# Attention with two feed-forward layers on one core: the softmax is moved from SBUF into the scores' PSUM banks

## Chip, core and metric

The kernel runs on one NeuronCore of a Trainium2 chip. The metric is the device time of one execution in microseconds (us). The engines are named as in the profile: PE is TensorE (matmuls; PEld is its loading of weights), DVE is VectorE, ACT is ScalarE, POOL is GpSimd and SP is SyncE, which here only issues DMAs. SBUF is the working memory that every engine reads; PSUM holds what PE writes, in eight banks of 512 fp32 columns for each of the 128 partitions. DVE and ACT can read and write PSUM. In this kernel POOL only ever touches SBUF.

## What is computed

```python
scores = q @ k.T / sqrt(64)                     # 4 x 8 heads, 576 x 576 each
cum = cumsum(log(clip(f, 1e-4, 1)))
scores = where(causal, -1e9, scores + cum[:, None] - cum[None, :])
attn = exp(scores - scores.max(-1)) ; attn /= attn.sum(-1) + 1e-9
x = (attn @ v) laid out as 2304 tokens x 512
x = leaky(x @ w_in) @ w_out                     # first layer, hidden 2048
h = x @ w2_in ; h = h * softmax(h)              # second layer, hidden 1024
out = (layernorm(h) * g_ln) @ w2_out
```

fp32 operands that are multiplied are split in a high and a low part, so that most products are three matmuls. The attention weights are split in fp16 the same way: `hl` holds the high and the low part of a block's rows.

## The kernel before

The 32 heads are worked in 16 pairs. Each head's scores fall into query blocks of 128 rows, 0 to 3, with 128, 256, 384 and 512 keys (causal); the last 64 rows of both heads of a pair make up a fifth block of 576 keys (`scores4`, block 4). Pairs 0 to 3 are done in two goes (blocks 0 and 1, then 2 to 4); pairs 4 to 15 in one go.

`scores` and `softmax` do one unit of blocks after the other; `UNITS` says which blocks share a unit. For each block PE writes scores into a bank `ps_s` (there are four). DVE adds the mask, takes the row maximum (L676, L695 for block 4) and writes the result to an SBUF tile `sd`, of which there are also four. From there all of it is in SBUF: ACT takes the exponential in place and its row sum (L641), a small instruction adds 1e-9 and scales (L649 on ACT, L651 on DVE or POOL), DVE takes the reciprocal (L654), and then come two large pieces per block:

```python
copy_f(hl.t[:, ho:ho + w], sd..., engs=HI_ENGS, scale=rs)    # high part, L425 ACT or L432 POOL
sub_f(hl.t[:, lo:lo + w], sd..., hl.t[:, ho:ho + w],
      engs=LO_ENGS if prio < LOP else ("DVE",), scale=rs)    # low part, L436 DVE or L439 + L440 POOL
```

A DMA transposes the unit's `hl` into `pt`, and PE multiplies it with the values (`ps_v`). ACT and DVE scale the result and add its two parts into `xr` (L706, L709). Around this run the preparation of keys and queries (`kq`, mostly POOL), of values (`VT`) and of weights (`wk`, four DVE instructions for each 128 x 512 chunk).

The first feed-forward layer is worked in nine token blocks. Its first half (`ffn_a`, nine hidden units of 12 matmuls each per token block, with g at L822 to L824) is interleaved with the attention as soon as a token block's attention output is there; the rest (`ffn_b`, `layer2`) follows.

Nothing of the order is decided on the chip. A planner (`Plan.run`) goes through all operations with costs written in the code, picks for each engine the operation of the best priority that is ready by those costs, chooses between engines where several are allowed, and hands out buffers. Each engine then executes its list in that order, and waits where an input or a buffer is late.

Of the kernel before, what the change touches and what calls it, by code (L numbers as in the profile page):

```python
# [24 lines left out]
PT = 4  # L25
# [29 lines left out]
LOP = 310.01  # L55
# [14 lines left out]
PS = 2.0 ** -15  # L70
# [25 lines left out]
HEAT = 0.25  # L96
# [260 lines left out]
def body(tc, kqa, kq, vt, f, one, wa, w2i, w2o, gln, out):  # L357
    nc = tc.nc
    es = ExitStack()
    P = Plan()  # L360
    PE, ACT, DVE, POOL, SP, CTL = "PE", "ACT", "DVE", "POOL", "SP", "CTL"
# [23 lines left out]
    ap = attn.enter_context(tc.tile_pool(name="attn", bufs=1))  # L385
# [168 lines left out]
    st, QK, VT, U, QA = {}, {}, {}, {}, {}  # L554
# [69 lines left out]
    def qk_mm(Q, full, i, o, hd, k0, k1, first, last):  # L624
        _, qk, col = Q
        c0 = col[i]
        if full:
            a = qk(hd)
            mm(o, a[0:66, c0:c0 + 128], a[0:66, k0:k1], first, last)
            return  # L630
        a, b = qk(hd)
        mm(o, a[:, c0:c0 + 128], a[:, k0:k1], first, False)
        mm(o, b[0:68, c0:c0 + 128], b[0:68, k0:k1], False, last)

    def softmax(parts, prio):
# [17 lines left out]
        flex(REC_ENGS, [{ACT: 100.0, DVE: 70.0, POOL: 165.0}[e] for e in REC_ENGS], guard, prio, w=[(sts, 3)], r=[(sts, 2)])  # L653
        P.op(DVE, 75, lambda: nc.vector.reciprocal(sts.t[:, 6:6 + nb], scale()), prio, w=[(sts, 4)], r=[(sts, 3)])  # L654
        for sd, _, j, W, pieces in parts:
            rs = lambda j=j: sts.t[:, 6 + j:7 + j]
# [89 lines left out]
    def pair(p, prio, blocks=(0, 1, 2, 3, 4)):  # L746
# [365 lines left out]
```

## Time and profile before

| | us |
|---|---|
| median of 3 runs | 887.11 (885.61 to 887.39) |
| the profiled execution | 887.7 |
| its span, first to last instruction | 885.9 |
| PE busy | 792.5 |
| DVE busy | 611.3 |
| ACT busy | 462.3 |
| POOL busy | 419.2 |

The span is what the trace covers; the profiled execution's own time is 1.8 us longer. A busy share over the whole span mixes an attention stage (to about 385 us, when the last `xr` is written) with feed-forward stages in which PE is busy nearly all the time.

### The profile page before, as it was taken

What the parts mean: (1) busy time and instruction counts of PE and PEld (TensorE: products, weight loads), DVE (VectorE), ACT (ScalarE), POOL (GpSimd) and SP (SyncE); (2) the same over time, 40 slices, a digit from 0 to 9 for tenths busy, and PEclk for the clock granted to TensorE, in tenths of its full rate; (3) what the DMA queues carried; (4) which work ended last, traced back from release to release, by engine and by line L of the source; (5) the groups of instructions that cost most, each with busy time, mean ns of one, the idle gap of its engine ahead of it and who ended that gap; (6) DMA issues with size and microseconds to landing.
All of it is one profiled execution on the core that took longest, in us unless ns stands there. A gap on an engine that the chain in (4) does not pass through costs nothing.

```text
span 885.9 us, 15864 instructions
## 1 busy us (share of the span) xinstructions
PE 792.5 (89%) x5648; PEld 711.0 (80%) x5648; DVE 611.3 (69%) x1369; ACT 462.3 (52%) x1150; POOL 419.2 (47%) x475
## 2 busy tenths in 40 slices
PE   2576688888689889999999989999999999999997
PEld 2333487788579878999999989889889988998985
DVE  6999988999899999958947896424533354234651
ACT  4776586776778878844435444333433342323421
POOL 5888886787676776233302345121412142223321
PEclk9999999999589999999999999999999999999999
DMA  7889569987878897855532532311422141203113
GB/s 214 208 193 222 153 169 184 199 212 166 202 179 194 179 222 200 155 165 167 178 110 87 164 119 60 79 41 60 86 56 62 36 107 36 60 30 80 24 36 95
DMA packets 181961, 114.98 MB, mean 130 GB/s; under 512 B 147030, under 2 KB 163054, under 8 KB 181850
## 3 DMA queue, kind: packets, MB, share of 16 engines
q1 hardware_dynamic: 181882, 113.97, 52.8%
q8 instruction: 44, 0.72, 0.3%
q14 instruction: 35, 0.29, 0.1%
HBM read 64.32 MB, written 15.16 MB: 90 GB/s over the span
## 4 chain that ended last, share of the span: by engine, by line
PE 45%; DVE 16%; issue 4%; ACT 4%; DMA 4%; POOL 1%; SPq 0%; DVEq 0%; ACTq 0%; POOLq 0%
PE ps_f L471 27%; PE ph L471 10%; PE py L471 6%; DVE hl L436 4%; DMA tr<-hl 2%; DVE wk L779 1%; DVE g L824 1%; DVE sd L676 1%; DVE xr L709 1%; PE ps_v L471 1%; DVE wk L781 1%; PE ps_s L471 1%; DMA raw<-w2o 1%; DVE wk L776 1%; ACT sd L641 1%
## 5 line engine op out<-in xcount | busy, mean ns | idle before, releaser
L436 DVE SCALAR_TENSOR_TENSOR hl<-sd,st,hl 128x512 f16<-128x512 f32 (+4 forms) x140 | 125.0, 907 | 8.4 <-POOL hl L432 6.0
L471 PE MATMUL ps_f<-x,wi 128*128 128x256 f32 x972 | 127.8, 287 | 1.6 <-DVE g L824 1.4
L471 PE MATMUL ps_f<-g,wo 128*128 128x256 f32 x972 | 126.1, 286 | 1.8 <-DVE g L824 1.8
L471 PEld LDWEIGHTS ps_f<-x,wi 128*128 128x128 f32 x972 | 122.9, 192 | 3.7 <-DVE g L824 2.5
L471 PEld LDWEIGHTS ps_f<-g,wo 128*128 128x128 f32 x972 | 121.6, 191 | 2.9 <-DVE g L824 2.5
L641 ACT ACTIVATE sd<-sd,st 128x128 f32<-128x128 f32 (+4 forms) x144 | 83.3, 579 | 41.8 <-DVE st L676 32.4
L471 PE MATMUL ps_f<-x,wib 128*128 128x256 f32 x756 | 99.0, 282 | 2.7 <-DVE g L824 1.4
L471 PE MATMUL ph<-wi,g 128*128 128x512 f32 x408 | 98.3, 397 | 0.0
L471 PEld LDWEIGHTS ps_f<-x,wib 128*128 128x128 f32 x756 | 93.1, 189 | 4.1 <-DVE g L824 2.7
L471 PE MATMUL ps_s<-kq 68*128 68x288 f32 (+9 forms) x304 | 70.4, 357 | 27.0 <-DVE st L676 21.0
L471 PEld LDWEIGHTS <-VT 128*128 128x128 f16 x928 | 56.6, 109 | 45.1 <-issue 32.1
L471 PE MATMUL ps_v<-pt,VT 128*128 128x128 f16 (+1 forms) x928 | 65.3, 233 | 30.7 <-DVE xr L709 24.6
L822 ACT ACTIVATE g<-ps_f 128x256 fp32r<-128x256 f32 x144 | 54.3, 377 | 70.7 <-PE ps_f L471 70.1
L471 PEld LDWEIGHTS ph<-wi,g 128*128 128x128 f32 x408 | 76.1, 189 | 17.5
L471 PE MATMUL ps_f<-wo,x 128*128 128x512 f32 x348 | 84.0, 397 | 0.2 <-ACT x L425 0.2
L824 DVE TENSOR_TENSOR g<-ps_f,g 128x256 fp32r<-128x256 f32 x144 | 60.0, 417 | 34.1 <-ACT ps_f L823 32.7
L471 PEld LDWEIGHTS ps_s<-kq 128*128 128x128 f32 (+1 forms) x304 | 50.1, 209 | 35.6 <-DVE st L676 25.8
L440 POOL TENSOR_TENSOR kq<-raw,kq 64x576 fp32r<-64x576 f32 (+2 forms) x47 | 76.1, 1619 | 4.9 <-ACT kq L425 2.2
L471 PE MATMUL py<-g,wob 128*128 128x256 f32 x567 | 76.7, 280 | 1.5 <-DVE yo L900 1.5
L471 PEld LDWEIGHTS ps_f<-wo,x 128*128 128x128 f32 x348 | 64.8, 189 | 15.3 <-ACT x L425 0.4
L471 PEld LDWEIGHTS py<-g,wob 128*128 128x128 f32 x567 | 72.5, 188 | 3.6 <-ACT wk L775 1.7
L432 POOL TENSOR_SCALAR hl<-sd,st 128x128 f16<-128x128 f32 (+3 forms) x69 | 40.2, 588 | 51.6 <-DVE st L654 27.1
(147 smaller groups left out, 1363.3 us busy)
## 6 DMA issues: line engine op xcount, KB each, us to landing
raw<-kq SPq DMA_DIRECT2D x24, 608.0 KB
wst<-wa SPq DMA_DIRECT2D x17, 512.0 KB
raw<-wa SPq DMA_DIRECT2D x15, 512.0 KB
xw<-xs_d SPq DMA_DIRECT2D x24, 256.0 KB
yp_d<-yo SPq DMA_DIRECT2D x36, 128.0 KB
yw<-yp_d SPq DMA_DIRECT2D x18, 256.0 KB
out<-ot SPq DMA_DIRECT2D x18, 256.0 KB
vr<-vt SPq DMA_DIRECT2D x13, 320.0 KB
```

Of the source, the lines that this page charges most:

```text
L432: nc.gpsimd.tensor_scalar(o, i, 1.0 if scale is None else scale, 1.0, op0=ALU.mult, op1=ALU.mult)
L436: nc.vector.scalar_tensor_tensor(o, a, scale, b, op0=ALU.mult, op1=ALU.subtract)
L440: (nc.vector if eng == DVE else nc.gpsimd).tensor_tensor(o, a, b, op=ALU.subtract)
L471: nc.tensor.matmul(o, lhsT=l, rhs=r, start=start, stop=stop)
L641: P.op(ACT, act(W, 2), lambda sd=sd, j=j, W=W: nc.scalar.activation(sd.t[:, 0:W], sd.t[:, 0:W], AF.Exp, bias=sts.t[:, j:j + 1], scale=-1.0 ...
L676: P.op(DVE, dve(W) + 12, lambda i=i, j=j, W=W, ps=ps, sd=sd: nc.vector.tensor_tensor_reduce(sd.t[:, 0:W], ps.t[:, 0:W], mask[:, 384 - 128 ...
L709: P.op(DVE, dve(n) + 60, lambda: nc.vector.scalar_tensor_tensor(xr.t[a:a + 64, dst0:dst0 + n], ps.t[a:a + 64, c0:c1], u.t[a:a + 64], xr.t[ ...
L776: P.op(DVE, dve2(512), lambda: nc.vector.tensor_scalar(kf(), kf(), F64_LO, F64_HI, op0=ALU.max, op1=ALU.min), prio, rw=[k])
L779: P.op(DVE, dve(512), lambda: nc.vector.scalar_tensor_tensor(k.t, word(1), -0x40000000, k.t, op0=ALU.bitwise_and, op1=ALU.bitwise_or), pri ...
L781: P.op(DVE, dve(512), lambda: nc.vector.scalar_tensor_tensor(k.t, word(0), 29, k.t, op0=ALU.logical_shift_right, op1=ALU.bitwise_or), prio ...
L822: P.op(ACT, act(n, 0, True), lambda: nc.scalar.activation(g.t[:, 0, 0:n], h(), AF.Prelu, alpha=0.01), eprio, w=[(g, 0)], r=[ps])
L824: P.op(DVE, dve(n) + 60, lambda: nc.vector.tensor_tensor(g.t[:, 1, 0:n], h(), g.t[:, 0, 0:n].bitcast(F32), op=ALU.subtract), eprio, w=[(g, ...
```

## The change

The masked scores stay in their `ps_s` bank, and mask, exponential, high part and low part all read them there. Since POOL is left out, the high part can go to ACT or DVE and the low part to DVE alone. Blocks 0, 1 and 2 become one unit, with blocks 0 and 1 in one bank. Block 4 is cut at 512 keys (a full bank and 64 columns of another) where it was cut at 288, and its exponential becomes two instructions.

```diff
-HI_ENGS = ("ACT", "POOL")
-UNITS = {2: ((0, 1),), 3: ((3,), (2,)), 5: ((0, 3), (1, 2))}
+HI_ENGS = ("ACT", "DVE")
+UNITS = {2: ((0, 1),), 3: ((3,), (2,)), 5: ((3,), (0, 1, 2))}
...
-    P.tag("sd", tiles(ap, "sd", 4, [128, S], F32))
-    P.tag("hl", tiles(ap, "hl", 3, [128, 1280], F16))
+    P.tag("sd", tiles(ap, "sd", 3, [128, S], F32))
+    P.tag("hl", tiles(ap, "hl", 3, [128, 1536], F16))
...
-            P.op(ACT, act(W, 2), lambda sd=sd, j=j, W=W: nc.scalar.activation(
-                sd.t[:, 0:W], sd.t[:, 0:W], AF.Exp, bias=sts.t[:, j:j + 1], scale=-1.0, accum_out=sts.t[:, 2 + j:3 + j]), prio,
-                w=[(sts, 2)], rw=[sd], r=[(sts, j)])
+            P.op(ACT, act(W, 1, True) + 93, lambda view=view, j=j, k=k: nc.scalar.activation(
+                view(), view(), AF.Exp, bias=sts.t[:, j:j + 1], scale=-1.0, accum_out=sts.t[:, 3 + k:4 + k]), prio,
+                w=[(sts, 2)], rw=[ps], r=[(sts, j)])
...
-                       engs=HI_ENGS, scale=rs, w=[(hl, ho)], r=[sd, (sts, 4)])
+                       engs=HI_ENGS, scale=rs, psum=True, w=[(hl, ho)], r=[ps, (sts, 4)])
...
-                      lambda ho=ho, w=w: hl.t[:, ho:ho + w], w, prio, engs=LO_ENGS if prio < LOP else ("DVE",), scale=rs,
-                      w=[(hl, lo)], r=[sd, (sts, 4), (hl, ho)])
+                      lambda ho=ho, w=w: hl.t[:, ho:ho + w], w, prio, engs=(DVE,), scale=rs,
+                      w=[(hl, lo)], r=[ps, (sts, 4), (hl, ho)])
...
+            joint = i < 2 and len(unit) > 1
+            if i == 1 and joint:
+                at = 128
+            else:
+                ps, at = P.buf("ps_s"), 0
+            view = lambda at=at, W=W, ps=ps: ps.t[:, at:at + W]
...
-            P.op(DVE, dve(W) + 12, lambda i=i, j=j, W=W, ps=ps, sd=sd: nc.vector.tensor_tensor_reduce(
-                sd.t[:, 0:W], ps.t[:, 0:W], mask[:, 384 - 128 * i:512], -0.125, 3.0e38, ALU.add, ALU.min, sts.t[:, j:j + 1]),
-                prio, w=[sd, (sts, j)], r=[ps])
+            P.op(DVE, dve(W) + 130, lambda i=i, j=j, view=view: nc.vector.tensor_tensor_reduce(
+                view(), view(), mask[:, 384 - 128 * i:512], -0.125, 3.0e38, ALU.add, ALU.min, sts.t[:, j:j + 1]),
+                prio, w=[(sts, j)], rw=[key])
```

The planner's lists change all over. On DVE, in the middle of the attention stage, the kernel before reads and writes `sd` (`ps_s` is the scores' bank, `hl` the split weights, `st` a column of statistics, `g` a hidden unit of `ffn_a`):

```order
L676 ISA sd_119,st_121<-ps_s_164,mask 128x384
L676 ISA st_121 128x1
L428 CAST kq_1_145<-kq_0_144 64x640
L654 RECIPROCAL st_126<-st_126 128x2
L824 TENSOR_TENSOR g_846<-ps_f_158,g_846 128x256
L436 SCALAR_TENSOR_TENSOR hl_129<-sd_117,st_126,hl_129 128x128
L676 ISA sd_117,st_124<-ps_s_167,mask 128x128
```

At a like place of the changed kernel the same engine reads and writes the banks:

```order
L436 SCALAR_TENSOR_TENSOR hl_127<-ps_s_164,st_124,hl_127 128x128
L610 ISA VT_109,vs_115<-ps_f_158,mask 128x128
L610 ISA vs_115 128x1
L436 SCALAR_TENSOR_TENSOR hl_127<-ps_s_164,st_124,hl_127 128x256
L436 SCALAR_TENSOR_TENSOR hl_127<-ps_s_166,st_124,hl_127 128x384
L436 SCALAR_TENSOR_TENSOR hl_128<-ps_s_163,st_125,hl_128 128x512
L727 SCALAR_TENSOR_TENSOR xr_133<-ps_v_167,u_113,xr_133 64x64 x2
L692 ISA ps_s_164,st_120<-ps_s_164,mask 128x384
```

The low part now has one operand in SBUF (`hl`) where it had two, and the bank `ps_s_164` takes new scores only after the low parts of blocks 0 and 1 have read it.

On POOL, in the same stage, the kernel before has high parts (L432 `hl`) between the splits of keys and queries:

```order
L432 TENSOR_SCALAR hl_127<-sd_117,st_121 128x256
L432 TENSOR_SCALAR hl_127<-sd_120,st_121 128x384
L432 TENSOR_SCALAR hl_128<-sd_118,st_124 128x512
L440 TENSOR_TENSOR kq_0_142<-raw_82,kq_0_142 64x640
L440 TENSOR_TENSOR kq_1_145<-raw_81,kq_0_144 64x576
L440 TENSOR_TENSOR kq_0_144<-raw_81,kq_0_144 64x640
L432 TENSOR_SCALAR hl_129<-sd_119,st_125 128x128
```

The changed kernel leaves the splits and a few small statistics there:

```order
L439 TENSOR_SCALAR vr_105<-vr_105,vs_116 128x640
L440 TENSOR_TENSOR VT_108<-vr_105,VT_108 128x10x64
L656 TENSOR_SCALAR st_123<-st_123 128x3
L440 TENSOR_TENSOR kq_1_142<-raw_82,kq_0_141 64x576
L440 TENSOR_TENSOR kq_0_141<-raw_82,kq_0_141 64x640
L656 TENSOR_SCALAR st_125<-st_125 128x1
L432 TENSOR_SCALAR kq_0_143<-raw_81 128x1216
```

All high and low parts are gone from POOL: over the whole program 69 high and 20 low parts move to ACT and DVE. On ACT the high parts rise from 91 to 149, and 11 are on DVE. Before the last `xr` the lists of ACT and DVE hold 45 hidden units of `ffn_a` in the kernel before and 52 in the changed one.

## Rows read from the trace of the kernel before

**Rows 1.** The page: busy time, share of the span, instructions of each engine.
```profile
PE 792.5 (89%) x5648; PEld 711.0 (80%) x5648; DVE 611.3 (69%) x1369; ACT 462.3 (52%) x1150; POOL 419.2 (47%) x475
```

**Rows 2.** Stretches of the span: length, busy time by engine, PE clock, DMA share.
```profile
0.00:100.00 100.00, 56.82 (x192) 34.77 (x193) 89.92 (x210) 63.10 (x150) 76.50 (x85) 1.00 0.83 210
...
150.00:375.00 225.00, 196.89 (x1782) 184.79 (x1780) 209.88 (x564) 174.99 (x480) 152.12 (x154) 0.93 0.86 190
375.00:525.00 150.00, 143.21 (x1198) 140.95 (x1197) 110.02 (x192) 71.30 (x178) 45.24 (x47) 1.00 0.48 147
```

**Rows 3.** Whom PE waited for, 150 to 375 us: total, times, longest.
```profile
PE ps_s L471 <- DVE st L676: 18.6, 18, 3.8
PE ps_s L471 <- DVE st L695: 5.3, 3, 3.2
```

**Rows 4.** DVE's groups by shape, 150 to 385 us: busy, mean ns, idle before.
```profile
L436 DVE SCALAR_TENSOR_TENSOR hl<-sd,st,hl 128x512 f16<-128x512 f32 x34 | 38.6, 1137 | 0.1
L436 DVE SCALAR_TENSOR_TENSOR hl<-sd,st,hl 128x384 f16<-128x384 f32 x23 | 23.7, 1030 | 0.1
L709 DVE SCALAR_TENSOR_TENSOR xr<-ps_v,u,xr 64x512 f32<-64x512 f32 x24 | 17.9, 746 | 5.7 <-ACT xr L706 5.4
L436 DVE SCALAR_TENSOR_TENSOR hl<-sd,st,hl 128x256 f16<-128x256 f32 x23 | 16.5, 717 | 3.0 <-POOL hl L432 1.9 <-ACT hl L425 1.0
L676 DVE CUSTOM_DVE_ANT_0 sd<-ps_s,mask 128x512 f32<-128x512 f32 x22 | 15.0, 682 | 0.5
L436 DVE SCALAR_TENSOR_TENSOR hl<-sd,st,hl 128x128 f16<-128x128 f32 x22 | 14.7, 669 | 4.2 <-POOL hl L432 3.7 <-ACT hl L425 0.4
L436 DVE SCALAR_TENSOR_TENSOR hl<-sd,st,hl 128x64 f16<-128x64 f32 x11 | 10.1, 915 | 0.1
L709 DVE SCALAR_TENSOR_TENSOR xr<-ps_v,u,xr 64x64 f32<-64x64 f32 x24 | 6.8, 281 | 3.5 <-ACT xr L706 3.1
```

**Rows 5.** POOL's four largest groups of `hl`, 150 to 385 us.
```profile
L432 POOL TENSOR_SCALAR hl<-sd,st 128x512 f16<-128x512 f32 x16 | 12.3, 768 | 6.9 <-DVE st L654 4.7 <-ACT sd L641 1.7 <-ACT hl L425 0.2
L432 POOL TENSOR_SCALAR hl<-sd,st 128x384 f16<-128x384 f32 x12 | 7.1, 593 | 10.3 <-issue 3.1 <-DVE st L654 2.0 <-DVE st L651 2.0
L432 POOL TENSOR_SCALAR hl<-sd,st 128x128 f16<-128x128 f32 x13 | 5.2, 400 | 17.8 <-DVE st L654 8.9 <-issue 4.8 <-DVE vs L613 1.9
L432 POOL TENSOR_SCALAR hl<-sd,st 128x256 f16<-128x256 f32 x9 | 5.1, 564 | 11.8 <-DVE st L654 6.7 <-ACT sd L641 2.3 <-issue 1.4
...
```

**Rows 6.** Timeline around 149 and 230 us: start, duration, engine, line.
```profile
149.24 2.09 DVE L436 SCALAR_TENSOR_TENSOR hl<-sd,st,hl 128x512 f16<-128x512 f32 x1
149.24 1.54 POOL L440 TENSOR_TENSOR kq<-raw,kq 64x640 fp32r<-64x640 f32 x1
...
229.32 0.69 DVE L676 CUSTOM_DVE_ANT_0 sd<-ps_s,mask 128x512 f32<-128x512 f32 x1
...
233.08 0.73 DVE L436 SCALAR_TENSOR_TENSOR hl<-sd,st,hl 128x512 f16<-128x512 f32 x1
```

**Rows 7.** ACT's groups by shape, 150 to 385 us, with SBUF and PSUM sources.
```profile
L706 ACT ACTIVATE xr<-ps_v,u 64x512 f32<-64x512 f32 x24 | 16.4, 683 | 3.5 <-PE ps_v L471 3.0
L425 ACT ACTIVATE hl<-sd,st 128x512 f16<-128x512 f32 x17 | 12.1, 713 | 5.5 <-DVE st L654 2.7 <-DMA pt<-hl 2.0 <-ACT xr L706 0.7
L706 ACT ACTIVATE xr<-ps_v,u 64x64 f32<-64x64 f32 x24 | 7.4, 309 | 1.9 <-DVE xr L709 1.3 <-PE ps_v L471 0.2
```

**Rows 8.** Whole trace, ACT's two writes of a hidden unit: to SBUF, to PSUM.
```profile
L822 ACT ACTIVATE g<-ps_f 128x256 fp32r<-128x256 f32 x144 | 54.3, 377 | 70.7 <-PE ps_f L471 70.1
L823 ACT ACTIVATE ps_f<-ps_f 128x256 f32<-128x256 f32 x144 | 53.9, 374 | 0.0
```

**Rows 9.** Chain that ended last: start, duration, one hidden unit's matmuls.
```profile
283.17 1.43 PE ps_f L471 x12
```

**Rows 10.** Instructions on `hl`, 0 to 150 us: busy time of DVE, ACT, POOL.
```profile
0.00:150.00 150.00, 23.84 (x28) 17.60 (x33) 30.48 (x35) 1.00 0.79 193
```

**Rows 11.** DVE's writes of `xr` over the trace: min, median, max ns; first, last.
```profile
L709 DVE SCALAR_TENSOR_TENSOR xr<-ps_v,u,xr x72: 264/467/758, 31.1 to 383.5; 64x64 f32<-64x64 f32 x32, 64x512 f32<-64x512 f32 x24, 64x256 f32<-64x256 f32 x16
```

More of the change, by code (lines that the diff above doesn't have):

```diff
@@ L639, in softmax @@
         hl, pt = P.buf("hl"), P.buf("pt")
-        for sd, _, j, W, pieces in parts:
-            P.op(ACT, act(W, 2), lambda sd=sd, j=j, W=W: nc.scalar.activation(
-                sd.t[:, 0:W], sd.t[:, 0:W], AF.Exp, bias=sts.t[:, j:j + 1], scale=-1.0, accum_out=sts.t[:, 2 + j:3 + j]), prio,
-                w=[(sts, 2)], rw=[sd], r=[(sts, j)])
-        total, scale = lambda: sts.t[:, 2:2 + nb], lambda: sts.t[:, 4:4 + nb]
+        one = parts[0][2] == parts[-1][2]
+        for k, (view, _, j, W, pieces, ps) in enumerate(parts):
+            P.op(ACT, act(W, 1, True) + 93, lambda view=view, j=j, k=k: nc.scalar.activation(
+                view(), view(), AF.Exp, bias=sts.t[:, j:j + 1], scale=-1.0, accum_out=sts.t[:, 3 + k:4 + k]), prio,
+                w=[(sts, 2)], rw=[ps], r=[(sts, j)])
+        ns = 1 if one else nb
+        total, scale = lambda: sts.t[:, 3:3 + ns], lambda: sts.t[:, 6:6 + ns]
         def guard(e):
-            if e == ACT:
+            if one and nb == 2:
+                nc.vector.scalar_tensor_tensor(scale(), total(), 1.0e-9, sts.t[:, 4:5], op0=ALU.add, op1=ALU.add)
+                nc.vector.tensor_scalar(scale(), scale(), PS, None, op0=ALU.mult)
+            elif e == ACT:
                 nc.scalar.activation(scale(), total(), CP, scale=PS, bias=1.0e-9 * PS)
@@ L651, in guard @@
                 (nc.vector if e == DVE else nc.gpsimd).tensor_scalar(scale(), total(), 1.0e-9, PS, op0=ALU.add, op1=ALU.mult)
[L653 to L656, printed above, removed]
+        engs = (DVE,) if one and nb == 2 else REC_ENGS
+        flex(engs, [{ACT: 100.0, DVE: 70.0 * nb, POOL: 165.0}[e] for e in engs], guard, prio, w=[(sts, 3)], r=[(sts, 2)])
+        P.op(DVE, 75, lambda: nc.vector.reciprocal(sts.t[:, 9:9 + ns], scale()), prio, w=[(sts, 4)], r=[(sts, 3)])
+        for view, _, j, W, pieces, ps in parts:
+            rs = lambda j=j: sts.t[:, 9 + j:10 + j]
             for ho, lo, so, w in pieces:
-                copy_f(lambda ho=ho, w=w: hl.t[:, ho:ho + w], lambda so=so, w=w, sd=sd: sd.t[:, so:so + w], w, prio,
-                       engs=HI_ENGS, scale=rs, w=[(hl, ho)], r=[sd, (sts, 4)])
+                copy_f(lambda ho=ho, w=w: hl.t[:, ho:ho + w], lambda so=so, w=w, view=view: view()[:, so:so + w], w, prio,
+                       engs=HI_ENGS, scale=rs, psum=True, w=[(hl, ho)], r=[ps, (sts, 4)])
             for ho, lo, so, w in pieces:
-                sub_f(lambda lo=lo, w=w: hl.t[:, lo:lo + w], lambda so=so, w=w, sd=sd: sd.t[:, so:so + w],
-                      lambda ho=ho, w=w: hl.t[:, ho:ho + w], w, prio, engs=LO_ENGS if prio < LOP else ("DVE",), scale=rs,
-                      w=[(hl, lo)], r=[sd, (sts, 4), (hl, ho)])
+                sub_f(lambda lo=lo, w=w: hl.t[:, lo:lo + w], lambda so=so, w=w, view=view: view()[:, so:so + w],
+                      lambda ho=ho, w=w: hl.t[:, ho:ho + w], w, prio, engs=(DVE,), scale=rs,
+                      w=[(hl, lo)], r=[ps, (sts, 4), (hl, ho)])
                 n += 2 * w
@@ L668, in scores @@
     def scores(p, unit, hd, prio, full):
-        sts, parts, n = P.buf("st"), [], 0
+        sts, parts, n, at = P.buf("st"), [], 0, 0
         for j, i in enumerate(unit):
-            ps, sd = P.buf("ps_s"), P.buf("sd")
             W = 128 * (i + 1)
-            P.op(PE, 4 * W / 2.4 if full else 2 * mmr(W), lambda Q=QK[p], i=i, W=W, ps=ps: qk_mm(
-                Q, full, i, ps.t[:, 0:W], hd, 0, W, True, True), prio, w=[ps], r=QK[p][0][hd], heat=HEAT if full else 1.0)
-            P.op(DVE, dve(W) + 12, lambda i=i, j=j, W=W, ps=ps, sd=sd: nc.vector.tensor_tensor_reduce(
-                sd.t[:, 0:W], ps.t[:, 0:W], mask[:, 384 - 128 * i:512], -0.125, 3.0e38, ALU.add, ALU.min, sts.t[:, j:j + 1]),
-                prio, w=[sd, (sts, j)], r=[ps])
-            parts.append((sd, sts, j, W, [(n, n + W, 0, W)]))
-            n += 2 * W
+            joint = i < 2 and len(unit) > 1
[4 more added lines that the diff above has]
+            view = lambda at=at, W=W, ps=ps: ps.t[:, at:at + W]
+            key = (ps, j) if joint else ps
+            P.op(PE, 4 * W / 2.4 if full else 2 * mmr(W), lambda Q=QK[p], i=i, W=W, view=view: qk_mm(
+                Q, full, i, view(), hd, 0, W, True, True), prio, r=QK[p][0][hd], heat=HEAT if full else 1.0,
+                **({"rw": [ps]} if at else {"w": [ps]}))
+            parts.append([view, sts, j, W, [(n, n + W, 0, W)], key, i])
+            n += 2 * W
+        for view, _, j, W, _, key, i in parts:
+            P.op(DVE, dve(W) + 130, lambda i=i, j=j, view=view: nc.vector.tensor_tensor_reduce(
+                view(), view(), mask[:, 384 - 128 * i:512], -0.125, 3.0e38, ALU.add, ALU.min, sts.t[:, j:j + 1]),
+                prio, w=[(sts, j)], rw=[key])
+        parts = [x[:6] for x in parts]
         pt = softmax(parts, prio)
@@ L684, in scores4 @@
     def scores4(p, prio, full):
-        pa, pb, sts, sd = P.buf("ps_s"), P.buf("ps_s"), P.buf("st"), P.buf("sd")
+        pa, pb, sts = P.buf("ps_s"), P.buf("ps_s"), P.buf("st")
         bq = QK[p][0]
-        for ps, k0, k1, init in ((pa, 0, S // 2, 3.0e38), (pb, S // 2, S, None)):
+        parts = []
+        for ps, k0, k1, init in ((pa, 0, 512, 3.0e38), (pb, 512, S, None)):
             def pe(ps=ps, k0=k0, k1=k1, Q=QK[p]):
@@ L694, in scores4 @@
             P.op(PE, 8 * n / 2.4 if full else 4 * mmr(n), pe, prio, w=[ps], r=bq[0] + bq[1], heat=HEAT if full else 1.0)
-            P.op(DVE, dve(n), lambda ps=ps, k0=k0, k1=k1, init=init: nc.vector.tensor_tensor_reduce(
-                sd.t[:, k0:k1], ps.t[:, 0:k1 - k0], mask4[:, k0:k1], -0.125, sts.t[:, 1:2] if init is None else init,
+            P.op(DVE, dve(n) + 130, lambda ps=ps, k0=k0, k1=k1, n=n, init=init: nc.vector.tensor_tensor_reduce(
+                ps.t[:, 0:n], ps.t[:, 0:n], mask4[:, k0:k1], -0.125, sts.t[:, 1:2] if init is None else init,
                 ALU.add, ALU.min, sts.t[:, 0:1] if init is None else sts.t[:, 1:2]),
-                prio, r=[ps, (sts, 1)] if init is None else [ps],
-                w=[(sd, k0), (sts, 0) if init is None else (sts, 1)])
-        return softmax([(sd, sts, 0, S, [(0, 512, 0, 512), (1024, 1088, 512, 64)])], prio)
+                prio, r=[(sts, 1)] if init is None else [], rw=[ps],
+                w=[(sts, 0) if init is None else (sts, 1)])
+            parts.append((lambda ps=ps, n=n: ps.t[:, 0:n], sts, 0, n,
+                          [(0, 512, 0, 512)] if k0 == 0 else [(1024, 1088, 0, 64)], ps))
+        return softmax(parts, prio)
     def evac(p, hd, ps, xr, c0, c1, dst0, prio):
```

4 lines of the change are left out of this document (2 added, 2 removed).

## The prediction

> **What bounds the kernel now.** I read the page's busy shares first: PE is busy 89% of the span [rows 1], so a gain can only come from the 93 us in which it is not, and from stretches with a low clock. The table of stretches says where these are. From 0 to 100 us PE is busy 57 us, from 150 to 375 us 197 of 225, from 375 to 525 us 143 of 150 [rows 2]. The middle one is the attention stage proper. There DVE is busy 209.9 of 225 us (93%), ACT 175.0 (78%), POOL 152.1, the DMA engines 86% and PE, at a mean granted clock of 0.93, 87.5%. So DVE ends most waits there, and the list of waits agrees: PE stands 18.6 and 5.3 us before `ps_s` matmuls because DVE has not yet masked the scores out of the bank [rows 3]. These are 24 of the stage's 28 idle PE microseconds.
>
> What DVE does in that stage is seen in its groups. The low part is the largest: 34, 23, 23, 22 and 11 instructions, together 103.6 us [rows 4]. Its durations are odd: 64 columns take 915 ns and 256 take 717. The timeline shows why: one 512-column low part takes 2.09 us while a POOL split that starts with it runs for 1.54 us, and another of the same shape takes 0.73 us [rows 6]. Both operands of L436 lie in SBUF, and it is held up by POOL. L709 is the same instruction with one operand in PSUM; it takes 746 ns for 512 columns and 281 for 64 in the same stage, with POOL as busy around it [rows 4], and never more than 758 [rows 11].
>
> **The change, part by part, in 150 to 375 us.**
>
> *Low parts.* They become L709's kind: one operand in PSUM, one in SBUF. A line through its two shapes gives 746, 613, 480, 347 and 281 ns for 512, 384, 256, 128 and 64 columns. Times the counts of [rows 4]: 25.4 + 14.1 + 11.0 + 7.6 + 3.1 = 61.2 us for 103.6. DVE sheds 42 us. [...]
>
> *Masks.* Some 113 mask instructions now write PSUM where they wrote SBUF (682 ns for 512 columns, [rows 4]). No row shows DVE writing PSUM. For ACT the destination is worth nothing (374 ns to PSUM, 377 to SBUF, [rows 8]); on the other side I bound it by the fixed part of the instruction itself, 682 less 512 columns at L709's slope of 1.04 ns, some 150 ns. That is 0 to 17 us; I take 8, the middle, since ACT's row is another engine's.
>
> *High parts.* In the stage POOL has 16, 12, 9 and 13 of them with 512, 384, 256 and 128 columns [rows 5]. On ACT from PSUM, L706 gives 683 ns for 512 and 309 for 64 columns [rows 7], so 576, 469 and 362 between: 10.9 + 6.9 + 4.2 + 4.7 = 27 us more for ACT. The few 64-column ones go to DVE, with other scraps at most 3 us. ACT's own pieces gain 30 ns each by the new source (713 against 683, [rows 7]); over some 160 exponentials and high parts that is 5 us, which the 11 additional instructions for block 4's tail (309 ns and a read of the sum each) eat again. ACT: 175 + 27 = 202 us.
>
> *POOL* loses those pieces, and it was not the bound. It waited for the reciprocal before them [rows 5]. The splits that stay compete less with DVE, a gain for the remaining SBUF instructions that I leave out of the sum.
>
> *Order.* 52 hidden units stand before the last `xr`, where 45 stood. Seven units are 7 x 1.43 = 10 us of PE [rows 9] that moves into the stage, and they cost ACT 7 x 0.75 = 5 us [rows 8].
>
> *Sum for the stage.* DVE falls from 210 to 210 - 42 + 8 + 3 = 179 us and would let it shrink by 31 us. ACT rises to 202 + 5 = 207 us. If ACT ran at 95%, a little above DVE's present 93%, the stage would take 218 us: 7 shorter, and with the 10 us of PE work that it takes along, 17. ACT's share need not be a wall, as the durations that I added overlap at their ends, so I go a little way towards the 31: **20 us**.
>
> *0 to 150 us.* DVE is full here as well (89.9 of the first 100 us, [rows 2]), but the balance is another: POOL spends 30.5 us on `hl` [rows 10], and its 20 low parts all move to DVE. At L709's prices they are some 11 us; DVE's own 28 low parts fall from 23.8 us to about 14, and 58 masks at 70 ns add 4. That is nothing, within a few us either way, covered by weight preparation that no longer meets as much POOL work. I take 0.
>
> *After 375 us.* Nothing in it changes. The weight preparation on DVE (110 of 150 us, [rows 2]) comes under a PE that is ahead by 20 us, so a few us could return; it starts earlier as well, and I book nothing.
>
> **Sum.** The profiled span of 885.9 less 20 is 865.9; with the 1.8 us around it 867.7; the median lies 0.6 below the profiled execution: **867 us**.
>
> **Rivals.**
>
> *DVE's relief goes through whole.* ACT has gaps to fill, the PE clock no longer falls (0.93 over 225 us is up to 15 us of rate, of which a good part is in the same gaps), and the gain is 31 to 45 us: 842 to 856. For it speaks that ACT's high parts waited on DVE [rows 7]; against it, that three engines and the DMA would all be above 85% in fixed lists. 0.20.
>
> *ACT takes it all.* At 207 us of work it can't go above the share it would have at the old pace, 92%, and only part of the moved PE work counts: 2 to 9 us, 878 to 885. 0.07. *No change* to within 0.2% (1.8 us, what a measurement of this kernel can tell): 0.05.
>
> *The banks become the bound* (slower). Before, a bank was free again after the mask, and four `sd` tiles held the rest. Now a bank is held from the scores to the last low part, and the next scores stand in PE's list with feed-forward matmuls behind them; everything behind waits. A pair uses 1 + 2 banks for each head and 2 for block 4: 8 uses on 4 banks. Twelve pairs (24 writes of 512 columns, [rows 4]) take 235 us, 19.6 us each, so the banks allow a mean hold of 9.8 us. From mask to the end of the low part I read 229.32 to 233.81, 4.5 us [rows 6]; the matmul, its wait in PE's list and the longer chain of the three-block unit (three masks, exponentials, high parts) add perhaps 2.5 to 4, so 7 to 8.5. It decides above 9.8: at 10.9 a pair takes 21.8 us, 12 pairs 26 us more, less the 10 us of PE work that moved in: 903, and 889 to 915 around it. [...] 0.14.
>
> *The low parts don't get cheaper* (the change does not do this part). If L436 stayed at 1.1 us because something other than POOL holds it, DVE would only gain work: 8 + 3 in the stage and 15 before, 889 to 905. Against it stands L709, undisturbed in the same stage. 0.04.
>
> **How the numbers follow.** The forecast, with 856 to 878, has 0.50. Faster by more than 0.2%: 0.50 + 0.20 + 0.07 = 0.77; same 0.05; slower 0.14 + 0.04 = 0.18. For the range I leave out the lower end of the full relief (about 0.04) and the upper two thirds of the slower cases (about 0.12): 844 to 891. The forecast's own range is 856 to 878.
>
> **What would show it.** Right: low parts at 0.75 us for 512 columns whatever POOL does; DVE's share from 150 us on clearly below 93% and ACT's at 88% or more; the last `xr` before 378 us in spite of seven more hidden units; PE's waits before `ps_s` below 24 us and its clock above 0.93. Wrong: masks at 0.83 us would take DVE's gain down by 17 us; `ps_s` matmuls that wait for a low part, more than 30 us in all, mean the banks; unchanged low parts mean that POOL was not the cause.

## The result, and the profile after

The changed kernel takes 876.16 us (median of 4 runs, 875.05 to 876.76) where the kernel before took 887.25 in the same session: ratio 0.9876, 95% interval 0.9857 to 0.9894. It is 11.1 us faster; 20 had been forecast. The page's first line, to be laid beside [rows 1]:

```profile
PE 791.8 (91%) x5648; PEld 706.2 (81%) x5648; DVE 581.2 (67%) x1405; ACT 477.8 (55%) x1221; POOL 343.1 (39%) x394
```

The same matmuls; DVE has 30 us less to do, POOL 76 less, ACT 15.5 more. The span fell by 12.6 us, from 885.9 to 873.3. The stretches say where (columns as in [rows 2]):

```profile
0.00:100.00 100.00, 54.38 (x185) 31.08 (x186) 88.31 (x216) 60.05 (x152) 52.27 (x57) 1.00 0.86 216
100.00:150.00 50.00, 46.41 (x368) 40.34 (x367) 43.35 (x135) 40.13 (x110) 30.21 (x32) 1.00 0.78 163
150.00:375.00 225.00, 205.66 (x1860) 193.23 (x1859) 185.53 (x577) 189.41 (x537) 112.14 (x108) 0.95 0.87 191
375.00:525.00 150.00, 143.81 (x1177) 140.42 (x1177) 118.26 (x206) 73.61 (x181) 48.20 (x53) 1.00 0.46 141
125.00:200.00 75.00, 74.29 (x704) 71.57 (x702) 60.85 (x206) 65.92 (x191) 46.53 (x42) 1.00 0.90 194
200.00:250.00 50.00, 35.13 (x263) 30.78 (x263) 42.30 (x126) 38.65 (x107) 29.82 (x32) 0.76 0.91 209
250.00:375.00 125.00, 121.23 (x1135) 115.27 (x1134) 102.71 (x318) 106.73 (x305) 52.20 (x51) 1.00 0.85 183
```

The kernel before in the stretches that [rows 2] does not have:

```profile
100.00:150.00 50.00, 40.96 (x337) 37.53 (x337) 45.70 (x116) 34.73 (x93) 41.77 (x37) 1.00 0.69 160
125.00:200.00 75.00, 65.96 (x610) 60.48 (x608) 69.85 (x181) 55.77 (x159) 57.67 (x52) 1.00 0.87 186
200.00:250.00 50.00, 37.13 (x289) 33.85 (x288) 45.07 (x116) 34.20 (x90) 35.18 (x35) 0.75 0.84 186
250.00:375.00 125.00, 116.27 (x1089) 111.04 (x1089) 118.17 (x326) 103.09 (x286) 80.47 (x86) 0.98 0.85 189
```

The first engine column is PE. It is busy 8.8 us longer in the attention stage (205.66 against 196.89), 5.4 longer from 100 to 150 us, 0.6 longer from 375 to 525, and 2.4 shorter in the first 100 us. That is 12.4 of the 12.6 us. The lower rows cut the stage in three. From 125 to 200 us PE is now full (74.29 of 75), from 250 to 375 nearly (121.23 of 125), but between 200 and 250 us it stands for 15 us, 2 more than before, and there neither DVE (42.30 of 50) nor ACT (38.65) is full. The granted clock falls there too, to 0.76 (0.75 before).

These two rows do not hold the same work. In the dip PE has no matmul of the first feed-forward layer: none runs between 199.66 and 237.58 us now, and none between 218.67 and 245.44 us before. The score matmuls (`ps_s`) in these stretches, the kernel before first (length, PE busy and count, clock, DMA):

```profile
218.67:245.44 26.77, 10.02 (x34) 0.63 0.84 189
199.66:237.58 37.92, 15.12 (x48) 0.72 0.85 203
```

Both are 1.27 score matmuls per us. So where PE has only attention to do, the attention came no faster than before; and PE runs out of first-layer work 19 us sooner while the next comes 8 us sooner, so this stretch is 11 us longer.

Some of DVE's and ACT's groups from 150 to 385 us, as in [rows 4] and [rows 7]:

```profile
L436 DVE SCALAR_TENSOR_TENSOR hl<-ps_s,st,hl 128x512 f16<-128x512 f32 x33 | 24.7, 747 | 4.2 <-ACT hl L425 3.6
L692 DVE CUSTOM_DVE_ANT_0 ps_s<-ps_s,mask 128x512 f32<-128x512 f32 x22 | 15.4, 701 | 2.7 <-PE ps_s L471 2.6
L436 DVE SCALAR_TENSOR_TENSOR hl<-ps_s,st,hl 128x384 f16<-128x384 f32 x23 | 14.0, 608 | 0.1
L692 DVE DVE_READ_ACCUMULATOR2_ANT st<- 128x1 f32 x88 | 12.1, 137 | 0.1
L436 DVE SCALAR_TENSOR_TENSOR hl<-ps_s,st,hl 128x256 f16<-128x256 f32 x23 | 10.9, 473 | 0.5 <-ACT hl L425 0.5
L436 DVE SCALAR_TENSOR_TENSOR hl<-ps_s,st,hl 128x128 f16<-128x128 f32 x23 | 8.0, 348 | 5.1 <-ACT hl L425 4.9
L436 DVE SCALAR_TENSOR_TENSOR hl<-ps_s,st,hl 128x64 f16<-128x64 f32 x11 | 3.1, 279 | 0.1
...
L642 ACT ACTIVATE ps_s<-ps_s,st 128x512 f32<-128x512 f32 x33 | 21.8, 660 | 5.4 <-DVE st L692 5.3
```

The same view of the kernel before, two groups that had not been shown (the mask's read of its accumulator, and the exponential in SBUF):

```profile
L676 DVE DVE_READ_ACCUMULATOR2_ANT st<- 128x1 f32 x89 | 7.1, 80 | 0.0
...
L641 ACT ACTIVATE sd<-sd,st 128x512 f32<-128x512 f32 x22 | 15.8, 716 | 9.5 <-DVE st L676 9.3
```

The low parts sum to 60.7 us. A mask of 512 columns with its read takes 838 ns, 76 more than before. What PE waited for, in the first 100 us and then from 150 to 375 (whom, total, times, longest):

```profile
PE ps_s L471 <- DVE hl L436: 17.8, 8, 5.6
...
PE ps_v L471 <- DVE xr L727: 5.6, 2, 3.6
```

```profile
PE ps_s L471 <- DVE hl L436: 10.8, 9, 3.7
PE ps_v L471 <- DMA pt<-hl: 3.9, 7, 0.9
```

The waits for the mask [rows 3] have become waits for the low part, as the last reader of a bank. 9.8 of the 10.8 us lie between 200 and 250 us. The last `xr` (min, median, max ns; first and last start) is no earlier than in [rows 11], but 52 hidden units stand before it where 45 did:

```profile
L727 DVE SCALAR_TENSOR_TENSOR xr<-ps_v,u,xr x72: 265/468/758, 34.5 to 383.4; 64x64 f32<-64x64 f32 x32, 64x512 f32<-64x512 f32 x24, 64x256 f32<-64x256 f32 x16
```

One bank in the middle stretch, row by row (timeline; in brackets the idle time before, and what ended it):

```profile
201.29 1.56 POOL L440 TENSOR_TENSOR kq<-raw,kq 64x640 fp32r<-64x640 f32 x1
...
201.44 1.42 DVE L651 SCALAR_TENSOR_TENSOR st<-st 128x1 f32<-128x1 f32 x1
...
201.68 1.18 PE L471 MATMUL ps_s<-kq 128*128 128x512 f32 x6
...
204.87 0.70 DVE L692 CUSTOM_DVE_ANT_0 ps_s<-ps_s,mask 128x512 f32<-128x512 f32 x1
...
205.71 0.66 ACT L642 ACTIVATE ps_s<-ps_s,st 128x512 f32<-128x512 f32 x1
...
206.54 1.01 PE L471 MATMUL ps_s<-kq 128*128 128x384 f32 x2 [3.69 <-DVE hl L436]
...
209.75 0.69 ACT L724 ACTIVATE xr<-ps_v,u 64x512 f32<-64x512 f32 x1 [1.26 <-PE ps_v L471]
210.46 0.69 ACT L425 ACTIVATE hl<-ps_s,st 128x512 f16<-128x512 f32 x1
...
211.59 0.73 DVE L436 SCALAR_TENSOR_TENSOR hl<-ps_s,st,hl 128x512 f16<-128x512 f32 x1
...
212.38 0.44 PE L471 MATMUL ps_s<-kq 128*128 128x128 f32 x2 [2.10 <-DVE hl L436]
```

The bank written at 201.68 is masked at 204.87, exponentiated at 205.71, copied at 210.46, and free at 212.32, after 10.6 us. The six instructions on it (mask, read, exponential, read, high part, low part) take 3.1 us of that. The rest is order: DVE had other work first (its guard L651, the sum that is made before the reciprocal, alone took 1.42 us), and ACT's high part stood behind an `xr` that itself waited for PE. PE then had no first-layer matmul to put between. So PE, ACT and DVE waited for each other in turn.

That hold is one of the longer ones. With first writes and last reads matched by shape and order in the timeline, the 88 holds of the last eleven pairs are 9.1 us on the mean (4.5 to 14.2). By this estimate 8 uses on 4 banks fill 18.2 of the 20.2 us that a pair takes.

### The profile page after: what moved, and what is told of

It reads as the page before. It is cut to its first block, busy times and chain, and to the rows that moved or that the text cites. A ratio compares the mean times of both kernels' runs of the same rounds, so it can differ in the third digit from the quotient of the medians.

```text
span 873.3 us, 15789 instructions
## 1 busy us (share of the span) xinstructions
PE 791.8 (91%) x5648; PEld 706.2 (81%) x5648; DVE 581.2 (67%) x1405; ACT 477.8 (55%) x1221; POOL 343.1 (39%) x394
## 4 chain that ended last, share of the span: by engine, by line
PE 48%; DVE 4%; DMA 3%; ACT 2%; issue 1%; POOL 0%; SPq 0%; ACTq 0%; DVEq 0%
PE ps_f L471 29%; PE ph L471 11%; PE py L471 7%; DMA raw<-wa 1%; DMA tr<-hl 1%; DVE wk L799 1%; DMA raw<-w2o 1%; DVE g L842 1%; PE ps_v L471 0%; DVE wk L795 0%; PE ps_s L471 0%; DVE x L440 0%; ACT wk L793 0%; DVE wk L794 0%; DVE raw L953 0%
## 5 line engine op out<-in xcount | busy, mean ns | idle before, releaser
L471 PEld LDWEIGHTS ps_f<-g,wo 128*128 128x128 f32 x972 | 119.8, 188 | 2.8 <-DVE g L842 2.4
L642 ACT ACTIVATE ps_s<-ps_s,st 128x512 f32<-128x512 f32 (+4 forms) x160 | 79.1, 494 | 23.6 <-DVE st L692 13.4
L436 DVE SCALAR_TENSOR_TENSOR hl<-ps_s,st,hl 128x512 f16<-128x512 f32 (+4 forms) x160 | 82.0, 538 | 15.0 <-ACT hl L425 13.6
L471 PE MATMUL ps_s<-kq 128*128 128x512 f32 (+9 forms) x304 | 72.7, 362 | 13.8 <-DVE hl L436 11.7
L425 ACT ACTIVATE hl<-ps_s,st 128x512 f16<-128x512 f32 (+4 forms) x149 | 74.2, 536 | 18.7 <-DVE st L660 11.3
L471 PEld LDWEIGHTS ps_s<-kq 128*128 128x128 f32 (+1 forms) x304 | 53.4, 209 | 23.0 <-DVE hl L436 16.1
```

The costliest lines, as they stand in the source:

```text
L425: nc.scalar.activation(o, i, CP, scale=1.0 if scale is None else scale)
L436: nc.vector.scalar_tensor_tensor(o, a, scale, b, op0=ALU.mult, op1=ALU.subtract)
L642: P.op(ACT, act(W, 1, True) + 93, lambda view=view, j=j, k=k: nc.scalar.activation(view(), view(), AF.Exp, bias=sts.t[:, j:j + 1], scale=- ...
```

## Experiments

The theory after the result: the low parts got cheap because one operand left SBUF, and the gain is smaller than forecast because the stage, once DVE has room, runs at the pace of the chain scores, mask, exponential, high part, low part, next scores through four banks, and not at that of the fullest engine. Rivals: the saving comes from POOL's absence alone; the planner's new list, and not the cheaper work, made the gain (or lost part of it); ACT or DVE alone is the bound. In the ratios below the kernel before is the one run beside the experiment.

**e1: other units.** The same PSUM softmax with the units of before, so that blocks 1 and 0 no longer share a bank (10 bank uses for a pair, not 8).

```diff
-UNITS = {..., 5: ((3,), (0, 1, 2))}
+UNITS = {..., 5: ((0, 3), (1, 2))}
-            joint = i < 2 and len(unit) > 1
+            joint = i < 2 and unit[:2] == (0, 1)
```

> The changed kernel with the units of before, blocks 0 and 3 and blocks 1 and 2, each block in a bank of its own: 10 bank uses for a pair where the change has 8. If the banks set the pace where PE has no feed-forward work (200 to 250 us), the dip there grows: 882 to 890 us, with PE's waits before scores above 30 us after 150 us. If the gain comes from the cheaper low parts and the banks are not tight, the units don't matter: 874 to 879 us.

887.95 us against 886.73 (1.0015, 1.0002 to 1.0029). The low parts are as cheap (747 ns), PE waits 33.1 us for them before 400 us (30.5 in the changed kernel), and the last `xr` comes at 398.9. With these units the change is worth nothing. Of the bank theory's two signs the time came, the waits above 30 us after 150 us did not (12.7). That the two more uses of a bank for each pair cost the 12 us is not shown: PE's waits grew by 2.6 us only, and the list changed too (54 units before the last `xr`), which alone can move the time by as much (e9, e10).

**e2: POOL left out, softmax in SBUF.** The kernel before with the engines of the changed one.

```diff
-HI_ENGS = ("ACT", "POOL")
+HI_ENGS = ("ACT", "DVE")
-                      ..., engs=LO_ENGS if prio < LOP else ("DVE",), scale=rs,
+                      ..., engs=("DVE",), scale=rs,
```

> The kernel before, softmax in SBUF, but with high parts on ACT or DVE and low parts on DVE alone. Theory A, the gain is that a PSUM source keeps low parts clear of POOL: here they keep two SBUF operands and still meet POOL's splits, 512 columns at 0.9 to 1.1 us, DVE has 20 more of them, 888 to 905 us. Rival C, leaving POOL is enough: low parts fall to about 0.75 us and the time to 875 to 880 us.

892.24 against 886.73: slower, 1.0074 (1.0052 to 1.0095). Two of its groups, whole trace:

```profile
L436 DVE SCALAR_TENSOR_TENSOR hl<-sd,st,hl 128x512 f16<-128x512 f32 x48 | 55.2, 1149 | 0.8 <-ACT hl L425 0.5
...
L436 DVE SCALAR_TENSOR_TENSOR hl<-sd,st,hl 128x64 f16<-128x64 f32 x16 | 11.7, 734 | 0.1
```

64 columns still take 734 ns (279 in the changed kernel). The high and low parts are gone from POOL, the splits that [rows 6] shows beside a slow low part are not; it is the operand in PSUM that frees the low part, not POOL's relief.

**e3: only the planner's costs.** The kernel before, with DVE's low parts booked at 380 ns more, near to what they take. No piece of work changes, only order and choice of engine.

```diff
-        d = {DVE: dve(n) + (60 if scale else 0), POOL: ...}
+        d = {DVE: dve(n) + (60 if scale else 0) + late, POOL: ...}     # late=380.0 in the low part
```

> The kernel before with one number changed: the planner books 380 ns more for each low part on DVE (about what the trace has above the planner's cost), so the list holds 54 hidden units before the last attention output, not 45. Nothing is computed in another way. Theory A: DVE still does the same slow work, 884 to 892 us. Rival B, the gain is only that the list fits the time and PE finds feed-forward work to do: 873 to 880 us.

879.11 against 886.73 (0.9918, 0.9896 to 0.9940). Another list alone gives 7.6 us, two thirds of what the change gave. It is not order alone, though. The low parts on DVE, in the kernel before and in e3:

```profile
L436 DVE SCALAR_TENSOR_TENSOR hl<-sd,st,hl 128x512 f16<-128x512 f32 (+4 forms) x140 | 125.0, 907 | 8.4 <-POOL hl L432 6.0
```

```profile
L436 DVE SCALAR_TENSOR_TENSOR hl<-sd,st,hl 128x128 f16<-128x128 f32 (+3 forms) x122 | 102.4, 866 | 4.9 <-POOL hl L432 3.4
```

With the higher cost the planner gave 18 low parts to POOL, and DVE's busy time fell from 611.3 to 597.7 us: this list, too, relieves DVE. From here on, a difference between kernels with different lists could not be read as the cost of an edit.

**e4: three banks.** The changed kernel with one bank unused.

```diff
-    P.tag("ps_s", tiles(ps_a, "ps_s", 4, [128, 512], F32))
+    P.tag("ps_s", tiles(ps_a, "ps_s", 3, [128, 512], F32))
+    tiles(ps_a, "ps_x", 1, [128, 512], F32)
```

> The changed kernel with three score banks, the fourth left unused. If a bank's hold sets the pace of the attention (8 uses for a pair), a quarter less banks makes the attention stage up to a third longer where it is bound by them: 900 to 940 us. If ACT or DVE work sets it, 876 to 885 us.

927.97 against 886.73: 1.0480 (1.0454 to 1.0505), 52 us above the changed kernel; the last `xr` moves to 435.2. Its stretch from 250 us on:

```profile
250.00:375.00 125.00, 112.96 (x965) 106.23 (x966) 88.25 (x277) 97.27 (x273) 55.52 (x54) 0.92 0.70 167
```

With three banks nothing is full: DVE 71%, ACT 78%, PE 90%. The list changed here too, but 52 us is three times the 16 us that lists alone make (e9, e10), so the banks are the likely pace there. PE's waits for low parts before 400 us hardly grew (30.5 to 33.8 us); what grew is the time that a pair takes, from 20.2 to 24.2 us, of which 8 holds of 8.2 us on 3 banks fill 22.0 by the estimate above. The mean granted clock was lower as well, 0.952 (0.986 in the changed kernel).

**e5, e6: a bank more.** A fifth bank had to come from the three `ps_f`. e5 takes `ps_f` to two and leaves the bank unused, e6 gives it to `ps_s`; in both a tile of the second layer that used to take over the third `ps_f` gets a bank of its own.

```diff
-    P.tag("ps_f", tiles(psum, "ps_f", 3, [128, 512], F32))
+    P.tag("ps_f", tiles(psum, "ps_f", 2, [128, 512], F32))
-    P.tag("ps_s", tiles(ps_a, "ps_s", 4, [128, 512], F32))      # e6 only
+    P.tag("ps_s", tiles(ps_a, "ps_s", 5, [128, 512], F32))      # e6 only
```

> Control for the next run: the changed kernel with two feed-forward banks where it has three, four score banks, and one bank left unused until phase 2. Feed-forward units wait more for ACT and DVE to empty a bank: 880 to 900 us. Alone it decides nothing.

> The same with the unused bank as a fifth score bank. If the banks' hold sets the attention's pace (three banks cost 52 us against four), a fifth gives part of it back: 8 to 20 us faster than the control, and the last attention output is earlier by 10 us or more. If four are enough and ACT, DVE or the list set the pace: within 4 us of the control.

e5: 888.29 against 887.28 (1.0015, 0.9994 to 1.0036). e6: 893.05 (1.0073, 1.0046 to 1.0099). e6 fell outside both of its expectations: the gain that I expected of the fifth bank did not come. e6's middle and late stretch:

```profile
200.00:250.00 50.00, 42.59 (x323) 37.62 (x322) 41.83 (x134) 41.49 (x116) 32.51 (x33) 0.73 1.06 215
250.00:375.00 125.00, 117.31 (x1076) 112.35 (x1075) 96.01 (x300) 100.89 (x292) 54.66 (x56) 0.96 0.83 180
```

PE is busier from 200 to 250 us, 42.59 (37.46 in e5), its waits for low parts before 400 us are 17.8 (22.4 in e5), and the last `xr` comes at 378.0 (382.2). But only 45 hidden units stand before the last `xr` (49 in e5), and PE is emptier after 250 us (117.31; 121.77 in e5). The waits moved with the banks as the theory has it; the time did not, and with the lists different it settles nothing. The mean hold, by the estimate above, grew to 11.1 us: holds stretch to the banks there are, so that full banks alone prove no bound.

**e7, e8: the same list, more work.** A repeat of up to 128 columns behind every low part on DVE (e7), or behind every high part on ACT (e8), not booked in the planner, so that every engine's list is that of the changed kernel with the repeats between. They do part of the softmax twice.

```diff
+                nc.vector.scalar_tensor_tensor(o[:, 0:m], a[:, 0:m], scale, b[:, 0:m], ...)    # e7, m = min(128, width)
+                nc.scalar.activation(o[:, 0:m], i[:, 0:m], CP, scale=scale)                    # e8
```

> The changed kernel, same lists, but DVE does the first 128 columns (64 for the short ones) of each low part twice: about 0.35 us more for each of 113 low parts after 150 us, 38 us of DVE, what the change took off it. The planner doesn't see it. Theory A, the relief of DVE carries the gain: 885 to 895 us, back to before or worse. Rival B, the list carries it and DVE's relief adds little: 877 to 881 us, as the run with changed costs alone.

> The same with ACT: the first 128 columns of each high part twice, 0.36 us for each of about 104 after 150 us, 37 us of ACT. If ACT is the next bound (the forecast's reason for a gain below DVE's relief), this costs more than the run with DVE: 890 us and more. If ACT has slack (84% busy), 877 to 884 us.

e7: 910.30 against 887.28 (1.0272, 1.0245 to 1.0298); e8: 906.07 (1.0217, 1.0199 to 1.0236). What was added in e7, in e8, and then the stretch from 250 us on of e7 and of e8:

```profile
L439 DVE SCALAR_TENSOR_TENSOR hl<-ps_s,st,hl 128x128 f16<-128x128 f32 x144 | 50.5, 351 | 5.1
...
L439 DVE SCALAR_TENSOR_TENSOR hl<-ps_s,st,hl 128x64 f16<-128x64 f32 x16 | 4.5, 284 | 0.6
```

```profile
L428 ACT ACTIVATE hl<-ps_s,st 128x128 f16<-128x128 f32 x142 | 52.2, 367 | 4.6
...
L428 ACT ACTIVATE hl<-ps_s,st 128x64 f16<-128x64 f32 x7 | 2.2, 313 | 0.2
```

```profile
250.00:375.00 125.00, 112.08 (x970) 102.95 (x970) 110.52 (x349) 100.34 (x286) 61.97 (x61) 0.94 0.78 175
```

```profile
250.00:375.00 125.00, 113.29 (x968) 105.42 (x968) 93.99 (x292) 114.35 (x332) 64.23 (x61) 0.93 0.78 171
```

55.0 us more on DVE lengthen the span by 34.4 us (907.7), 54.4 us more on ACT by 31.7 (905.0): 0.6 us for each us, whichever of the two engines gets it. (By the engines' busy time on the page, which counts overlaps once and rose by 44.7 us on DVE and 49.9 on ACT, it is 0.8 and 0.6.) Not all of it is waiting: for the same 5648 matmuls PE was busy 14.2 us longer in e7 (806.0) and 10.1 in e8 (801.9), at a granted clock of 0.89 and 0.90 from 150 to 375 us where it had been 0.95. e7 is slower than both of its expectations; e8 is slower than the 890 us that were to show ACT as the bound, but did not cost more than e7, as that also asked. Neither engine was full in the changed kernel (82% and 84% of the stage; 39 and 36 us free in it). With one engine as the bound, work for the other would first have filled such gaps; that both cost much the same speaks for one chain through both. PE's waits for low parts before 400 us grow from 30.5 to 49.2 (e7) and 38.0 us (e8). The stretch without first-layer matmuls, 37.92 us for 48 score matmuls in the changed kernel, is longer for the same 48 in e7 and in e8:

```profile
215.36:258.78 43.42, 17.24 (x48) 0.58 0.67 168
```

```profile
212.68:254.10 41.42, 15.18 (x48) 0.63 0.82 180
```

**e9, e10: other costs for the changed kernel.** e9 books masks and low parts (also 130 less) below what they take; e10 books weight preparation, splits without a scale and the guard nearer to what they take.

```diff
-            P.op(DVE, dve(W) + 130, ...                       # e9: the mask
+            P.op(DVE, dve(W) - 120, ...
-        P.op(DVE, dve2(512), ...                              # e10: weight preparation, +185 and +195
+        P.op(DVE, dve2(512) + 185, ...
```

> The changed kernel planned with the error that the kernel before had: for each block the planner books 380 ns less of DVE (250 at the mask, 130 at the low part), so its list holds 49 hidden units before the last attention output, not 52. The instructions are the same. If the list's fit carries the gain (rival B), it is lost: 884 to 892 us. If the cheaper low parts carry it (theory A), 875 to 880 us.

> The changed kernel with costs nearer to its trace for DVE work that still meets POOL: 185 or 195 ns more for each weight-preparation instruction, 250 ns more for each unscaled difference, 640 ns for block 4's guard. Rival B, a list that fits gains here too: 866 to 873 us, and the first 150 us have fewer waits before scores. If the list fits well enough already: 874 to 879 us.

e9: 872.09 against 886.48 (0.9830, 0.9805 to 0.9855). e10: 888.06 (1.0010, 0.9989 to 1.0031). Both fell outside their expectations. Costs that fit better gave the slower list, costs that fit worse the faster one; in e3 it was the other way. Where e9's 4 us come from its profile can't tell: the profiled execution is its slowest (874.2), with a span of 872.4, and PE is 4.6 us busier in the first 100 us and 3.7 less in the next 50. Its stretch without first-layer matmuls is only 18.8 us long (212.10 to 230.86), but e11 below gains with one of 38.3. The same PSUM softmax takes 872 to 888 us by the list alone, which is order and choice of engine (in e10 POOL has 37.5 us more to do, 380.6 for 343.1).

**e11: the guard of block 4 in another form.** This form came with the change, when block 4's exponential became two instructions with a sum each. Its two operands of one column lie in SBUF; now one is a pointer scalar (one value per partition, read as the instruction's scalar). The list is the same.

```diff
-                nc.vector.scalar_tensor_tensor(scale(), total(), 1.0e-9, sts.t[:, 4:5], op0=ALU.add, op1=ALU.add)
+                nc.vector.tensor_scalar(scale(), total(), sts.t[:, 4:5], 1.0e-9, op0=ALU.add, op1=ALU.add)
```

> The changed kernel with one instruction in another form: block 4's sum of its two row sums (570 ns, two SBUF tensors, 16 times) takes the second sum as a per-partition scalar, with the same list. If it falls to about 0.15 us, the chain from block 4's exponential to its low parts is 0.4 us shorter, twelve times in the stage whose pace the banks set: 871 to 875 us. If block 4's banks don't set the pace: 875 to 877 us.

873.30 against 886.48 (0.9840, 0.9818 to 0.9863). DVE's group on this line over the whole trace, in the changed kernel and in e11:

```profile
L651 DVE SCALAR_TENSOR_TENSOR st<-st 128x1 f32<-128x1 f32 x16 | 9.1, 570 | 1.2 <-ACT ps_s L642 0.9
```

```profile
L651 DVE TENSOR_SCALAR st<-st 128x1 f32<-128x1 f32 x16 | 3.3, 207 | 1.2 <-ACT ps_s L642 1.1
```

5.8 us of DVE go, and 2.9 us of time by the medians; the intervals of the two ratios overlap, and the spans (872.4 and 873.3) are 0.9 apart. The cheaper guard is shown, its worth in time is not. The wait of 3.69 us above remains (3.94 at 206.21), so the 1.42 us guard was not what set it alone. In e11 the next DVE instruction there with two operands in SBUF, a low part of the values (`VT`), took 1.75 us beside the same POOL split, where it had taken 0.89 after the guard.

**e12: e9's costs and e11's guard together.**

> The changed kernel with e9's planner costs and e11's form of the guard instruction on block 4. Theory A (what an instruction on the chain between mask and low part costs is its excess duration, taken at about half, as 2.9 us for 16 x 0.36 us in e11): in e9's list the guard took 318 ns on the mean, 208 as a tensor_scalar, so 16 x 0.11 = 1.8 us of DVE go and about 0.9 us of time: 871.2 us (870 to 872.5), last xr at 378.5. Rival B (the gain of e11 is the same in any list, since it comes from the one instruction's place): 872.1 - 2.9 = 869.2 us (868 to 870). Rival C (the two gains do not add, since e11 removed the same stalls that e9's list avoids): 872 to 874. If A or B holds it is the fastest version of this study; A and C overlap within what the measurement can tell.

874.82 against 887.05 (0.9855, 0.9834 to 0.9876), and the guard takes 212 ns. That is a little above all three expectations, nearest to the last: the two gains do not add. e9, e11 and e12 lie 12 to 14 us below the kernel before with overlapping intervals, and e9's median is the lowest.

## Why the prediction came out as it did

*Low parts: right, in mechanism and size.* 60.7 us in place of [rows 4]'s 103.6, for 61.2 forecast; the longest in the whole trace took 754 ns. A 512-column piece took 747 ns from PSUM, with POOL busy 112 us in the stage; from SBUF it took 1149 over the whole of e2, with POOL busy 143 us in the stage.

*Masks: right.* 76 ns for 70. Three quarters of it is the read of the accumulator (137 ns for 80), the rest the mask (701 for 682). DVE as a whole came to 185.5 us in the stage, not 179: the hidden units that moved into it cost DVE 0.42 us each as well, which the sum had left out.

*High parts and ACT: direction right, size off.* ACT rose from 175.0 to 189.4 us, not to 207. Added one by one, its instructions in the stage grew by 22.3 us (205.3 to 227.6), of which 7.9 lie in overlaps. Hidden units brought it 3 us and not 5, exponentials of 512 columns became 56 ns shorter where 30 had been booked, and 4 us of value splits (`VT`) left its list. The share of 88% that was to show the forecast right did not come (84%).

*The step that failed is the sum for the stage:* "If ACT ran at 95%, a little above DVE's present 93%, the stage would take 218 us: 7 shorter, and with the 10 us of PE work that it takes along, 17", and then 20. The stage took the seven units along, and it did not get shorter: the last `xr` stands at 383.4 as at 383.5 before (the forecast's sign was before 378). So 8.8 us of the 20 came. Its other signs came true: DVE's share 82%, PE's waits before `ps_s` 12.6 us, the clock 0.95. I had divided busy time by a share over the whole stage, as if it were one regime. PE's idle time from 125 to 375 us was 30.6 us; 13.3 of it went outside the stretch from 200 to 250 us, where little is left now (0.7 and 3.8). Within that stretch it grew from 12.9 to 14.9, as PE now has nothing but attention for most of it; and the attention by itself came at the same 1.27 score matmuls per us as before. There the relief of DVE was worth nothing. That this is so because the chain through the banks passes through ACT and through the order of three lists as well is what e7 and e8 speak for; no run changed that stretch alone.

*0 to 150 us: booked at 0, in truth +5.4 and -2.4.* DVE's relief showed here as well: PE's waits before `ps_v` for DVE's `xr` fell from 6.4 to 0.4 us between 100 and 150 us, and from 16.5 to 5.6 in the first 100; but there 17.8 us before banks came in their place (5.9 before). That the median of 876.2 lies in the forecast's 856 to 878 is partly luck: without the 3.0 us that came from here it would be about 879.

*After 375 us: right* (0.6 us).

*The rival of the banks* was no bound of the whole, as the forecast had it, but it is the likely bound of the stretches that did not gain: a mean hold of 9.1 us, an estimate, where the forecast had 7 to 8.5, and 52 us for a bank less. Shown it is not: a fifth bank brought no time (e6), and the lists differ. Its sign, "more than 30 us in all", was not reached in the stage (10.8 us); over 0 to 400 us it stood at 30.5.

*What stays open:* how much of the 11.1 us is the cheaper work and how much the list that the planner happened to make. Lists alone moved the SBUF kernel by 7.6 us, with DVE relieved by another way, and the PSUM kernel by 16. That the work is cheaper is shown; that a us of DVE is worth 0.6 to 0.8 us was shown only upwards, by adding (e7). Whether a fifth bank would help under an unchanged list was not found out.

## What to carry to other kernels

Moving the working tile into PSUM turned the bank into the buffer of the whole chain here (the one followed above was held 10.6 us): count the uses of a bank and the time from first write to last read, other engines' queues included, before you divide busy time by a share. Look for stretches where PE has nothing else in its list, since an engine's relief was worth least there in this case. Where a planner orders the work, compare edits that leave the list as it is (add unbooked work, change an instruction's form), or the list's own scatter, here 16 us, hides what you ask for.

## What the runs showed of the hardware

- Reading the accumulator of a mask that wrote PSUM took 137 ns, of one that wrote SBUF 80.
- The exponential of 512 columns took 660 ns in place in PSUM and 716 in SBUF.
- A DVE instruction with two SBUF operands of a single column (the guard, 16 times in the changed kernel) took 150 to 160 ns eight times. The other eight times it ran beside a POOL instruction on SBUF tiles, took 479 to 1415 ns, and ended 10 to 21 ns after that instruction did, as in the first two rows of the bank's timeline. With the second operand as a pointer scalar (e11) it took 193 to 214 ns all 16 times; the one at 201.47 us, 0.20 us long, ran beside the 1.53 us of the same POOL split. So POOL held up even the smallest of these here, and the other form was not held up.
